# Sketched attention and a two-layer block: a new order for the first chunk, the first weight, chunk 1 and batch 1, and features in two column halves

## The chip, the cores and the metric

The kernel runs on one core of one Trainium2 chip. The metric is the device time of one execution in microseconds (us). Before the change three runs took 143.87, 144.07 and 145.85 us; the median is 144.07.

## The reference

Attention replaces the softmax by products of two sketches; a layer norm and a two-layer block with a residual follow. Inputs are q, k, v of 4 batches, 4 heads, 1088 rows and 32 columns, S1 and S2 of 8 x 32, and weights of 128 x 512 and 512 x 128.

```python
def phi(x):
    a = np.einsum('rd,bhsd->bhsr', S1, x)
    b = np.einsum('rd,bhsd->bhsr', S2, x)
    return np.einsum('bhsi,bhsj->bhsij', a, b).reshape(*x.shape[:-1], r * r)
q_p, k_p = (phi(q), phi(k))
kv = np.einsum('bhsf,bhsd->bhfd', k_p, v)
z = np.sum(k_p, axis=2)
num = np.einsum('bhsf,bhfd->bhsd', q_p, kv)
den = np.einsum('bhsf,bhf->bhs', q_p, z)[..., None] + 1e-06
x = num / den                                # then (B, S, H*D), 128 columns
mu = np.mean(x, axis=-1, keepdims=True)
var = np.mean((x - mu) ** 2, axis=-1, keepdims=True)
xn = (x - mu) / np.sqrt(var + 1e-06) * g_ln
ch = np.maximum(xn @ w_ch1, 0.0) @ w_ch2
out = x + ch
```

The sketches and the weights arrive as 64-bit numbers. The kernel turns them into 32-bit ones with integer and float steps on their two words.

## The kernel before

A batch is 9 tiles of 128 positions-by-head columns for keys. Queries are worked on in 9 chunks: two chunks of four tiles for each batch, and a last one with what is left of all batches. All engines are written in one program order; each engine runs its own instructions in the order of the program and waits on semaphores for the others. There is no planner: the order of the calls at the end of the kernel sets everything.

The steps by name. `turn_k(b, ..)` transposes keys on DVE. `sketches` turns S1 and S2 into the block matrix `sk` (two matmuls and a masked copy), and `sketches2` makes `s2b`. `key_features` multiplies the transposed keys with `sk` on PE (L289) and copies to `fs` on ACT (L291). `key_products` multiplies the two halves of `fs` into `kp`, on POOL or DVE (L298). `key_sums` (L309) and `key_scale` (L323) bring the sum of the key features into the third part of `skq`, the weights with which the queries are multiplied. `key_values` (L329) contracts `kp` with v, `key_rows` copies it, `key_spread` (L344) transposes it into `kvr`.

For a chunk c: `turn_q` transposes queries on DVE (L354), `query_features` multiplies with `skq` into the PSUM bank FB (L372, L377 for the last chunk) and copies to `fq` on ACT (L383). `quotients` (L396 to L401) makes the denominator and divides on DVE, `query_products` (L408) forms `qp`, `query_turn` (L420) transposes it to `qpT`, and `numerators` (L442) contracts it with `kvr` into X and copies to `xT` on ACT (L451). `rows_of` (L459, L461) turns `xT` into rows `x`, and `stats` (L468 to L475) takes mean and variance on DVE and the power on POOL. `hidden(c, j)` (L491, L492) is a quarter of the first layer with its relu on ACT, `second(c, t)` (L500) one tile of the second layer, `finish` (L511) adds the residual and stores.

The first weight is brought into 32 bits by DVE (`split`, `power`), ACT (three float steps) and POOL (`last`), and then multiplied with `cg`, the scale of the layer norm with the mean taken out (L566, L567). The second weight takes the same steps without the product.

PSUM holds X (four banks), M[0] and M[1] (the two layers take turns in them), XP and FB. `fill(n, w)` issues n products of a tile of ones into M[0], whose result nobody reads. In the trace each of these matmuls is two instructions.

The loads stand on one queue (SP's) in the order k of batch 0 in two pieces, w1, q of batch 0, v of batch 0, w2, then the other batches; S1 and S2 stand on ACT's queue, g on POOL's.

Before the change the whole of batch 0's keys, chunk 0 up to the rows, chunk 1 up to its products, both weights, and batch 1's keys up to the scale come ahead of the first `hidden`. From there a loop over the nine chunks mixes the dense layers of chunk c with the features of chunk c + 2, the numerators of chunk c + 1, and the next batch's key work.

Of the kernel before, what the change touches and what calls it, by code (L numbers as in the profile page):

```python
# [25 lines left out]
def kernel(  # L26
# [132 lines left out]
    def fill(n, w):  # L159
        for _ in range(n):  # L160
            pe.matmul(M[0][:, 0:w], ones, ones[:, 0:w], start=True, stop=True)  # L161
# [49 lines left out]
    class weight:  # L211
# [7 lines left out]
        def split(self):  # L219
            if not self.plain:  # L220
                split(self.t)
                t = self.t
                act.activation(t["exf"], t["ex"], AF.Relu, bias=m896)
                act.activation(t["mant"], t["bits"], AF.Identity, bias=one, scale=2.0**-20)
                act.activation(t["low"], t["lo"], AF.Copy, scale=2.0**-52)

        def power(self):
            if not self.plain:
                power(self.t, P)

        def last(self, eng=None):
            t = None if self.plain else self.t
            if self.plain:
                pool.tensor_copy(out=self.dst, in_=self.raw)
            else:
# [1 line left out]
                pool.tensor_tensor(out=self.dst, in0=t["mant"], in1=t["e3"].bitcast(F32),
                                   op=ALU.mult)
# [17 lines left out]
    def sketches():  # L256

        for i in range(2):
            pe.matmul(FB[:, R * i : R * (i + 1)],
                      s_f[:, DM * i : DM * (i + 1)], ident[0:R, 0:R],  # L260
                      start=True, stop=True)
        dve.tensor_tensor(
            out=_ap(sk, 0, P, 0, [[HR, 2], [R, H], [1, R]]),
            in0=_ap(FB, 0, P, 0, [[R, 2], [0, H], [1, R]]),
            in1=_ap(m32, 0, P, 0, [[0, 2], [1, H], [0, R]]),
            op=ALU.mult,
        )
# [18 lines left out]
    def key_features(b, t0, t1, bank):  # L286
        base = 512 * bank - W * t0
        for t in range(t0, t1):
            pe.matmul(X[:, base + W * t : base + W * (t + 1)],  # L289
                      kT[b % 2][:, P * t : P * (t + 1)], sk, start=True, stop=True)  # L290
        act.copy(  # L291
            _ap(fs[b % 2], 0, P, HR * t0, [[HR, t1 - t0], [KB, 2], [1, HR]]),
            _ap(X, 0, P, base + W * t0, [[W, t1 - t0], [HR, 2], [1, HR]]),
# [11 lines left out]
    def key_sums(b, o=1536):  # L305
        f = fs[b % 2]
        for t in range(NT):
            c = t % 4
            pe.matmul(  # L309
                X[32 * c : 32 * c + 32, o : o + 32],  # L310
# [11 lines left out]
    def key_scale(b, o=1568):  # L322
        pe.matmul(X[:, o : o + 32], s2b, zT, start=True, stop=True)  # L323
        dve.tensor_copy(out=skq[b][:, W : W + HR], in_=X[:, o : o + HR])  # L324
# [43 lines left out]
    def query_features(c):  # L368
        n = tiles(c)
        if c < 8:  # L370
            for t in range(n):
                pe.matmul(FB[:, WQ * t : WQ * (t + 1)], qT[c][:, P * t : P * (t + 1)],  # L372
                          skq[c // 2], start=True, stop=True)
        else:
            for t in range(n):
                for i in range(2):
                    pe.matmul(  # L377
# [284 lines left out]
```

## Time and profile before

| | |
|---|---|
| median of three runs | 144.07 us |
| the profiled execution | 144.32 us |
| its span, first to last instruction | 142.5 us |
| PE busy | 121.7 us, 85% of the span |
| DVE, ACT, POOL busy | 62.1, 43.7, 51.0 us |
| mean granted TensorE clock | 0.891 |
| first `hidden` product starts at | 42.69 us |

The profiled execution's own time is 1.8 us above its span; sums made on the trace have to be compared with 144.32 and not with the median. Busy PE time is modelled from pipelined matmuls, so it shows where PE has work and not how well it is used. A row of the timeline gives the start, the time from its first instruction's start to its last one's end, engine, line, and in brackets the idle time ahead and what ended it. The granted clock is a separate column of the windows.

### The profile page before, as it was taken

The page shows a single profiled execution, that of the slowest core. Times are in us where ns is not written, and L with a number is a line of the kernel's source. Part 1 is how long each engine was busy: PE and PEld are TensorE (multiplying, and loading weights), DVE is VectorE, ACT ScalarE, POOL GpSimd, SP SyncE. Part 2 cuts the span into 40 slices and gives each one's busy share as a digit, 9 for nine tenths or more (in the row PEclk, how much of TensorE's full clock was granted, in tenths as well). Part 3 has the DMA queues.
Part 4 walks back from the last instruction along what each step waited for, and adds up shares of the span by engine and source line. Part 5 has one row for each costly group of instructions (what it writes and reads, how often), then busy time and mean ns, then how long its engine had stood idle before and what let it go on. Part 6 is the DMA issues. An engine that isn't in the chain of part 4 may idle for free. (4 is left out here: it accounts for less than half of the span.)

```text
span 142.5 us, 3720 instructions
## 1 busy us (share of the span) xinstructions
PE 121.7 (85%) x1586; PEld 93.6 (66%) x1586; DVE 62.1 (44%) x208; ACT 43.7 (31%) x85; POOL 51.0 (36%) x61
## 2 busy tenths in 40 slices
PE   7789883392579999989999999999999999899750
PEld 7679872262466488569668757965966858569440
DVE  2704377009705558433456653365453544301310
ACT  4011116030611540532253254044236054142310
POOL 6242041605299503373650255545305320302000
PEclk9975589655555999999999999999999999999999
DMA  4899999980000000300020030020011030030111
GB/s 144 252 248 288 227 295 243 266 205 13 0 0 2 0 5 5 74 0 5 18 55 5 4 77 0 0 60 25 0 40 38 2 74 5 0 78 0 45 33 35
DMA packets 6273, 10.21 MB, mean 72 GB/s; under 512 B 1136, under 2 KB 3952, under 8 KB 6256
## 3 DMA queue, kind: packets, MB, share of 16 engines
q1 hardware_dynamic: 6000, 9.90, 27.9%
q8 instruction: 12, 0.20, 0.6%
q10 hardware_dynamic: 224, 0.07, 0.2%
q14 instruction: 5, 0.04, 0.1%
q0 software_dynamic: 32, 0.00, 0.0%
HBM read 7.74 MB, written 2.23 MB: 70 GB/s over the span
## 5 line engine op out<-in xcount | busy, mean ns | idle before, releaser
L491 PE MATMUL M<-xT,w 128*128 128x512 f32 (+1 forms) x72 | 37.5, 612 | 1.2 <-DVE ob L511 1.2
L492 ACT ACTIVATE hT<-M 128x512 f32<-128x512 f32 (+1 forms) x36 | 20.7, 574 | 49.6 <-PE M L491 49.5
L500 PE MATMUL M<-w,hT 128*128 128x128 f32 x272 | 33.4, 277 | 0.0
L500 PEld LDWEIGHTS M<-w,hT 128*128 128x128 f32 x272 | 31.8, 192 | 0.2
L408 POOL TENSOR_TENSOR qp<-a,fq 128x1024 f32<-128x1024 f32 (+1 forms) x9 | 16.2, 1803 | 35.2 <-DVE a L401 35.2
L289 PE MATMUL X<-sk,kT 128*128 128x64 f32 x72 | 12.5, 334 | 6.8 <-ACT fs L291 3.0
L289 PEld LDWEIGHTS X<-sk,kT 128*128 128x128 f32 x72 | 11.6, 244 | 8.7 <-ACT fs L291 3.6
L298 POOL TENSOR_TENSOR kp<-fs 128x1024 f32<-128x1024 f32 (+1 forms) x7 | 15.0, 2148 | 5.5 <-ACT fs L291 5.5
L491 PEld LDWEIGHTS M<-xT,w 128*128 128x128 f32 x72 | 11.6, 198 | 6.2 <-issue 2.6
L511 DVE SCALAR_TENSOR_TENSOR ob<-M,rstd,x 128x128 f32<-128x128 f32 x34 | 9.6, 343 | 13.8 <-PE M L500 9.8
L420 DVE STREAM_TRANSPOSE qpT<-qp 128x1024 f32<-128x1024 f32 (+1 forms) x10 | 10.7, 1079 | 10.6 <-POOL qp L408 10.6
L468 DVE BATCH_NORM_STATS2 st<-x 128x6 f32<-128x128 f32 x34 | 7.4, 278 | 15.9 <-ACT x L461 15.9
L372 PEld LDWEIGHTS FB<-skq,qT 128*128 128x128 f32 x64 | 10.8, 243 | 4.0 <-issue 3.3
L473 POOL TENSOR_SCALAR va<-mv 128x4 f32<-128x4 f32 (+1 forms) x9 | 2.1, 230 | 30.4 <-DVE mv L470 25.0
L442 PEld LDWEIGHTS X<-qpT,kvr 32*32 32x32 f32 x640 | 7.1, 103 | 8.5 <-issue 6.7
L442 PE MATMUL X<-qpT,kvr 32*32 32x128 f32 (+1 forms) x640 | 10.3, 262 | 1.3 <-DVE qpT L420 0.9
L372 PE MATMUL FB<-skq,qT 128*128 128x96 f32 x64 | 10.8, 327 | 0.4 <-DVE skq L324 0.4
L396 DVE TENSOR_TENSOR ac<-FB,fq 128x128 f32<-128x128 f32 (+1 forms) x9 | 2.6, 284 | 16.8 <-ACT fq L383 16.8
L161 PE MATMUL M<-ones 128*128 128x128 f32 x40 | 8.6, 390 | 1.0 <-DVE m L125 1.0
L475 POOL TENSOR_TENSOR rstd<-va,mhalf 128x4 f32<-128x4 f32 (+1 forms) x9 | 9.0, 1003 | 0.8
L161 PEld LDWEIGHTS M<-ones 128*128 128x128 f32 x40 | 7.7, 292 | 1.3 <-DVE m L125 1.0
L459 PEld LDWEIGHTS XP<-ident,xT 128*128 128x128 f32 x34 | 4.7, 151 | 5.4 <-issue 5.4
(80 smaller groups left out, 100.8 us busy)
## 6 DMA issues: line engine op xcount, KB each, us to landing
qn<-in_q_dram SPq DMA_DIRECT2D x4, 544.0 KB, 8.4
out_dram<-ob SPq DMA_DIRECT2D x32, 64.0 KB, 1.7
kn<-in_k_dram SPq DMA_DIRECT2D x3, 544.0 KB, 11.3
vn<-in_v_dram SPq DMA_DIRECT2D x8, 144.0 KB, 8.6
w_raw<-in_moe_w_ch_dram SPq DMA_DIRECT2D x2, 512.0 KB, 6.1
vn<-in_v_dram SPq DMA_DIRECT2D x8, 128.0 KB, 7.9
kn<-in_k_dram SPq DMA_DIRECT2D x1, 288.0 KB, 2.9
kn<-in_k_dram SPq DMA_DIRECT2D x1, 256.0 KB, 3.0
```

What stands on the lines that cost most here:

```text
L161: pe.matmul(M[0][:, 0:w], ones, ones[:, 0:w], start=True, stop=True)
L289: pe.matmul(X[:, base + W * t : base + W * (t + 1)], kT[b % 2][:, P * t : P * (t + 1)], sk, start=True, stop=True)
L298: eng.tensor_tensor(out=_ap(o, 0, P, H * F * t0, [[F, (t1 - t0) * H], [R, R], [1, R]]), in0=_ap(f, 0, P, HR * t0, [[R, (t1 - t0) * H], [1, ...
L372: pe.matmul(FB[:, WQ * t : WQ * (t + 1)], qT[c][:, P * t : P * (t + 1)], skq[c // 2], start=True, stop=True)
L408: eng.tensor_tensor(out=_ap(qp[c], 0, P, H * F * t0, [[F, m], [R, R], [1, R]]), in0=_ap(a2s[c], 0, P, H * R * t0, [[R, m], [1, R], [0, R]] ...
L420: dve.transpose(_ap(qpT[c], 0, P, 32 * t0, [[32, t1 - t0], [32 * n, 8], [1, 32]]), qp[c][:, t0 * H * F : t1 * H * F],)
L442: pe.matmul(X[D * h : D * h + D, o : o + 32 * m], kv[rows, DM * i + D * h : DM * i + D * h + D], t[rows, src : src + 32 * m], start=(i == ...
L475: pool.tensor_tensor(out=rs[:, 0:n], in0=va[:, 0:n], in1=mhalf[:, 0:n], op=ALU.pow)
L491: pe.matmul(hp[:, 0:n], w1[:, P * j : P * (j + 1)], xT[c][:, 0:n], start=True, stop=True)
L492: act.activation(hT[c][:, 512 * j : 512 * j + n], hp[:, 0:n], AF.Relu)
L500: pe.matmul(po[c][:, DM * t : DM * (t + 1)], hT[c][:, 512 * j + P * t : 512 * j + P * (t + 1)], w2[:, DM * j : DM * (j + 1)], start=(j == ...
L511: dve.scalar_tensor_tensor(out=ob[:, P * t : P * (t + 1)], in0=po[c][:, P * t : P * (t + 1)], scalar=rstd[c][:, t : t + 1], in1=x[c][:, P ...
```

## The change

*Features in two column halves.* A tile's 128 columns are multiplied as two matmuls of 64 columns that write the two halves of the partitions, in `key_features` and `query_features`. `key_features` of batches 1 to 3 is one block with one copy to `fs`; batch 0's two parts go to M[0] and M[1].

*Start.* S2 is loaded on SP's queue ahead of k, and q of batch 0 ahead of w1. `sketches` writes X in place of FB, and stands between the two key transposes. `cg` is made on POOL at the start, ahead of the four copies of `sk` into `skq`, which now stand ahead of the key products. Batch 0's key products all run on POOL, in three parts.

*First chunk.* Ones are multiplied at more places, 64 instructions in place of 40. `key_values` of batch 0 is cut into three parts with ones between them. `query_products(0)` runs on DVE in four instructions that read one factor from FB, so `fq` of chunk 0 needs only half its copy. `skq` and batch 0's `kvr` are copied by ACT.

*First weight.* It is split after zT and finished in two halves of 256 columns; `mean_free` multiplies each half with `cg`. The second half comes behind the first `hidden`.

*Chunk 1 and batch 1.* `hidden(0, 0)` follows the numerators of chunk 0. What stood ahead of it (chunk 1's features, rows of chunk 0, the second weight, batch 1's keys) is written between the dense products of chunks 0 and 1, by hand. The loop starts with chunk 2.

```diff
-    for i, src in enumerate((S1, S2)):
-        act.dma_start(out=s_raw[:, D * i : D * (i + 1)], in_=src)
+    act.dma_start(out=s_raw[:, 0:D], in_=S1)
+    nc.sync.dma_start(out=s_raw[:, D : 2 * D], in_=S2)
...
+    load_rows(qn, q, 0)
     nc.sync.dma_start(out=w1_raw, in_=moe_w_ch1)
-    load_rows(qn, q, 0)
...
-    def fill(n, w):
+    def fill(n, bank, w=P):
         for _ in range(n):
-            pe.matmul(M[0][:, 0:w], ones, ones[:, 0:w], start=True, stop=True)
+            pe.matmul(bank[:, 0:w], ones, ones[:, 0:w], start=True, stop=True)
...
-    def key_features(b, t0, t1, bank):
-        base = 512 * bank - W * t0
+    def key_features(b, t0=0, t1=NT, bank=None):
+        y = X if bank is None else bank
         for t in range(t0, t1):
-            pe.matmul(X[:, base + W * t : base + W * (t + 1)],
-                      kT[b % 2][:, P * t : P * (t + 1)], sk, start=True, stop=True)
+            for c in range(2):
+                pe.matmul(
+                    y[64 * c : 64 * c + 64, W * (t - t0) : W * (t - t0 + 1)],
+                    kT[b % 2][:, P * t + 64 * c : P * t + 64 * c + 64], sk,
+                    start=True, stop=True,
+                )
...
-        dve.tensor_copy(out=skq[b][:, W : W + HR], in_=X[:, o : o + HR])
+        act.copy(skq[b][:, W : W + HR], y[:, o : o + HR])
...
+        for t in range(n):
+            for i in range(2):
+                src, w = (qT[c], skq[c // 2]) if c < 8 else (qTr, skq[2 * t + i])
+                pe.matmul(
+                    FB[64 * i : 64 * i + 64, WQ * t : WQ * (t + 1)],
+                    src[:, P * t + 64 * i : P * t + 64 * i + 64], w,
+                    start=True, stop=True,
+                )
...
+    def mean_free(a, n, bank):
+        pe.matmul(bank[:, 0:n], cg, w1g[:, a : a + n], start=True, stop=True)
+        act.copy(w1[:, a : a + n], bank[:, 0:n])
+
+    pool.tensor_scalar(out=cg, in0=ident, scalar1=-1.0 / DM, scalar2=g_raw,
+                       op0=ALU.add, op1=ALU.mult)
+    fill(7, FB)
     turn_k(0, 0)
+    sketches()
     turn_k(0, 2)
...
-    for c in range(9):
+    for c in range(2, 9):
```

Three places of the new order, as each engine has them. The first is PE in the first chunk, from the key sums of batch 0 to the numerators of chunk 0: before,

```order
L309 MATMUL X<-fs_201 32x32 x9
L161 MATMUL M_70<-ones 128x128 x4
L323 MATMUL X<-zT,s2b 128x32
L372 MATMUL FB<-skq_197,qT 128x96 x4
L329 MATMUL X<-kp_203,vn_87 32x64 x36
L161 MATMUL M_70<-ones 128x128 x2
L344 MATMUL X<-ident,kvT 128x128 x2
L161 MATMUL M_70<-ones 128x128 x4
L442 MATMUL X<-qpT,kvr_207 32x128 x32
```

and now, from the query features on,

```order
L392 MATMUL FB<-skq_197,qT 64x96 x8
L161 MATMUL XP<-ones 128x128 x4
L344 MATMUL X<-kp_203,vn_87 32x64 x16
L161 MATMUL XP<-ones 128x128 x3
L344 MATMUL X<-kp_203,vn_87 32x64 x12
L161 MATMUL XP<-ones 128x128 x3
L344 MATMUL X<-kp_203,vn_87 32x64 x8
L161 MATMUL XP<-ones 128x128 x2
L360 MATMUL M_70<-ident,kvT 128x128 x2
L161 MATMUL XP<-ones 128x128 x2
L561 MATMUL M_71<-w1g,cg 128x256
L161 MATMUL XP<-ones 128x128 x2
```

The key values (L329, now L344) are in three parts with products on ones between, and the first half of the weight's product stands ahead of the numerators. The second place is PE behind the numerators of chunk 0: before,

```order
L442 MATMUL X<-qpT,kvr_207 32x128 x32
L566 MATMUL M_71<-w1g,cg 128x512
L459 MATMUL XP<-ident,xT 128x128 x4
L372 MATMUL FB<-skq_197,qT 128x96 x4
L289 MATMUL X<-sk,kT_148 128x64 x9
L309 MATMUL X<-fs_202 32x32 x9
L323 MATMUL X<-zT,s2b 128x32
L491 MATMUL M_71<-xT,w_177 128x512
```

and now

```order
L467 MATMUL X<-qpT,kvr_207 32x128 x32
L161 MATMUL XP<-ones 128x128 x2
L516 MATMUL M_71<-xT,w_177 128x512
L392 MATMUL FB<-skq_197,qT 64x96 x8
L561 MATMUL XP<-w1g,cg 128x256
L516 MATMUL M_70<-xT,w_177 128x512
L484 MATMUL XP<-ident,xT 128x128 x4
L516 MATMUL M_71<-xT,w_177 128x512
L516 MATMUL M_70<-xT,w_177 128x512
L301 MATMUL X<-sk,kT_148 64x64 x18
L467 MATMUL X<-qpT,kvr_207 32x128 x32
```

The first dense product (L491, now L516) stands two rows behind the numerators; batch 1's key features (L289, now L301) stand behind all four. The third place is DVE from the quotients of chunk 2 on, where qT holds the transposed queries of chunk 3: before,

```order
L396 TENSOR_TENSOR ac_157<-FB,fq 128x16x8
L398 TENSOR_REDUCE den<-ac_157 128x16
L400 RECIPROCAL rden<-den 128x16
L401 TENSOR_TENSOR a_465<-FB,rden 128x128
L354 STREAM_TRANSPOSE qT<-qn_84 128x4x4x32
L360 STREAM_TRANSPOSE qTr<-qn_84 128x64
L420 STREAM_TRANSPOSE qpT<-qp 128x4x8x32
L468 BN_STATS st<-x 128x6 x4
L470 BN_AGGR mv<-st 128x2 x4
```

and now

```order
L412 TENSOR_TENSOR ac_157<-FB,fq 128x16x8
L414 TENSOR_REDUCE den<-ac_157 128x16
L416 RECIPROCAL rden<-den 128x16
L417 TENSOR_TENSOR a_587<-FB,rden 128x128
L493 BN_STATS st<-x 128x6 x4
L495 BN_AGGR mv<-st 128x2 x4
L373 STREAM_TRANSPOSE qT<-qn_84 128x4x4x32
L412 TENSOR_TENSOR ac_158<-FB,fq 128x16x8
L414 TENSOR_REDUCE den<-ac_158 128x16
L416 RECIPROCAL rden<-den 128x16
L417 TENSOR_TENSOR a_625<-FB,rden 128x128
L445 STREAM_TRANSPOSE qpT<-qp 128x4x8x32
```

The statistics of chunk 1 stood behind chunk 2's products; now they stand ahead of the transposed queries of chunk 3 (L354, now L373), and the quotients of chunk 3 stand ahead of the transpose of chunk 2's products (L420, now L445).

More of the change, by code (lines that the diff above doesn't have):

```diff
@@ L267, in sketches @@
         )
+        for b in range(B):
+            pool.tensor_copy(out=skq[b][:, 0:W], in_=sk)
     def sketches2():
@@ L340, in key_rows, with key_spread @@
         )
-    def key_spread(b):
+    def key_spread(b, y=None, on_act=False):
+        y = X if y is None else y
         for i in range(2):
-            pe.transpose(X[:, P * i : P * (i + 1)], kvT[:, P * i : P * (i + 1)], ident)
-        dve.tensor_copy(out=kvr[b], in_=X[:, 0 : 2 * DM])
+            pe.transpose(y[:, P * i : P * (i + 1)], kvT[:, P * i : P * (i + 1)], ident)
+        if on_act:
+            act.copy(kvr[b], y[:, 0 : 2 * DM])
+        else:
+            dve.tensor_copy(out=kvr[b], in_=y[:, 0 : 2 * DM])
     qT = {}
@@ L549 @@
     query_features(0)
+    W1.floats(1, 0, 256)
+    W1.floats(2, 0, 256)
+    W1.power(0, 256)
     quotients(0)
[L551 to L564 removed]
+    fill(4, XP)
@@ L565 @@
+    key_values(0, 0, 4)
+    fill(3, XP)
+    W1.floats(0, 256, 256)
+    key_values(0, 4, 7)
+    fill(3, XP)
+    W1.floats(1, 256, 256)
+    W1.floats(2, 256, 256)
+    key_values(0, 7, 9)
+    W1.last(0, 256)
+    query_products(0, dve)
+    query_turn(0)
+    key_rows()
+    fill(2, XP)
+    key_spread(0, M[0], on_act=True)
+    fill(2, XP)
+    mean_free(0, 256, M[1])
+    fill(2, XP)
     numerators(0)
-    pe.matmul(M[1], cg, w1g, start=True, stop=True)
-    act.copy(w1, M[1])
+    W1.power(256, 256)
@@ L579 @@
-    W2.last()
-    key_features(1, 0, 4, 0)
-    key_features(1, 4, 9, 1)
-    key_products(pool, 1, 0, 4)
-    key_products(pool, 1, 4, 9)
-    key_sums(1)
-    key_scale(1)
-    turn_q(2)
-    stats(0)
-    for c in range(9):
+    key_features(1)
+    query_turn(1)
+    numerators(1)
+    key_products(pool, 1, 0, 4)
+    stats(0)
+    second(0, 0)
+    key_sums(1, X, 1536)
+    second(0, 1)
+    rows_of(1)
+    key_products(pool, 1, 4, 9)
+    second(0, 2)
+    key_scale(1, X, 1568)
+    turn_q(2)
@@ new lines @@
+    turn_q_rest(0)
+    second(0, 3)
+    query_features(2)
+    finish(0)
+    quotients(2)
+    query_products(2, pool)
+    stats(1)
+    hidden(1, 0)
+    turn_q(3)
+    query_features(3)
+    quotients(3)
+    query_products(3, pool)
+    hidden(1, 1)
+    query_turn(2)
+    key_values(1)
+    key_rows()
+    hidden(1, 2)
+    key_spread(1)
+    turn_k(2, 0)
+    turn_k(2, 2)
+    hidden(1, 3)
+    numerators(2)
+    second(1, 0)
+    key_features(2)
+    key_products(pool, 2, 0, 4)
+    second(1, 1)
@@ L590 @@
+    rows_of(2)
+    stats(2)
+    key_sums(2, X, 1536)
+    second(1, 2)
+    key_products(pool, 2, 4, 9)
+    query_turn(3)
+    key_scale(2, X, 1568)
+    turn_q(4)
+    turn_q_rest(1)
+    second(1, 3)
+    finish(1)
+    for c in range(2, 9):
         nb = c // 2 + 1 if c % 2 == 0 else c // 2 + 2
@@ L596 @@
             quotients(c + 2)
-            query_products(c + 2, pool, 0, tiles(c + 2))
+            query_products(c + 2, pool)
         hidden(c, 1)
```

157 lines of the change are left out of this document (80 added, 77 removed).

## The prediction

> **What bounds the kernel now.** The chain of waits ends in two output steps and unexplained issue time (3% of the span), so it says nothing of the middle. I read the windows instead, cut where the TensorE clock changes. The columns after the length are busy time with instruction counts for PE, weight loads, DVE, ACT and POOL, then the granted clock.
>
> ```profile
> 5.54:8.95 3.41, 1.87 (x14) 1.54 (x13) 1.74 (x4) 0.37 (x1) 0.02 (x1) 1.00 1.00 273
> 15.78:19.19 3.41, 3.41 (x79) 3.07 (x79) 1.58 (x5) 0.46 (x2) 0.33 (x1) 0.50 1.06 269
> 19.19:22.60 3.41, 2.51 (x69) 2.15 (x70) 2.72 (x7) 0.29 (x1) 1.17 (x1) 1.00 1.07 262
> ...
> 26.02:42.69 16.67, 9.93 (x53) 8.04 (x53) 6.19 (x13) 4.12 (x8) 7.50 (x5) 0.50 0.35 82
> 43.08:46.49 3.41, 3.41 (x11) 2.33 (x11) 1.67 (x10) 0.60 (x2) 3.24 (x3) 0.50 0.01 2
> 68.65:132.00 63.35, 62.53 (x937) 45.80 (x936) 28.47 (x104) 23.49 (x45) 22.02 (x20) 1.00 0.11 27
> ```
>
> From 68.65 to 132 PE is busy 62.53 of 63.35 us at full clock: PE is the bound there, and only less PE work helps. From 26.02 to 42.69 PE idles 6.7 us and works the rest at half clock. That stretch is the target. PE's own timeline there, and the first matmul of chunk 2's dense block:
>
> ```profile
> 27.23 2.08 PE L566 MATMUL M<-w1g,cg 128*128 128x512 f32 x2 [3.66 <-POOL w1g L237]
> 29.10 1.06 PE L459 MATMUL XP<-ident,xT 128*128 128x128 f32 x4
> 29.95 1.86 PE L372 MATMUL FB<-skq,qT 128*128 128x96 f32 x8
> 34.83 1.97 PE L289 MATMUL X<-sk,kT 128*128 128x64 f32 x8 [3.02 <-DVE kT L245]
> 38.45 2.39 PE L289 MATMUL X<-sk,kT 128*128 128x64 f32 x10 [1.65 <-ACT fs L291]
> 41.35 0.53 PE L309 MATMUL X<-fs 128*32 128x32 f32 x18 [0.52 <-ACT fs L291]
> 42.24 0.63 PE L323 MATMUL X<-zT,s2b 128*128 128x32 f32 x2 [0.35 <-DVE zT L315]
> 42.69 1.20 PE L491 MATMUL M<-xT,w 128*128 128x512 f32 x1
> ...
> 68.65 1.02 PE L491 MATMUL M<-xT,w 128*128 128x512 f32 x2
> ```
>
> PE waits 3.66 us for the first weight, then for batch 1's keys; the first dense product stands at 42.69, the first of chunk 2 at 68.65. The change puts the first dense product right behind chunk 0's numerators, and spreads batch 1's key work between the dense products of chunks 0 and 1. So I sum three pieces: T0, the new time of that first product; from T0 to chunk 2's first; and from there to the end.
>
> **T0.** The prologue's rows:
>
> ```profile
> 1.04 4.63 PE L161 MATMUL M<-ones 128*128 128x128 f32 x20 [1.04 <-DVE m L125]
> ...
> 4.33 0.18 DVE L174 TENSOR_SCALAR bitss<-s_raw 8x64 uint32<-8x64 uint32 x1 [1.11 <-DMA s_raw<-in_S_dram]
> ...
> 7.33 1.10 PE L289 MATMUL X<-sk,kT 128*128 128x64 f32 x8 [0.72 <-DVE sk L262]
> ...
> 14.97 1.99 PE L372 MATMUL FB<-skq,qT 128*128 128x96 f32 x8 [0.38 <-DVE skq L324]
> 16.89 2.15 PE L329 MATMUL X<-kp,vn 128*32 128x64 f32 x72
> ...
> 19.83 1.06 PE L161 MATMUL M<-ones 128*128 128x128 f32 x8
> 21.79 0.98 PE L442 MATMUL X<-qpT,kvr 32*32 32x128 f32 x55 [0.90 <-DVE qpT L420]
> ```
>
> A product on ones is two instructions: 0.23 us each at low clock (4.63/20), 0.13 at full (1.06/8). Two DMA queues carry S1 and S2 instead of one in turn; I take 0.5 us off (between nothing and 0.9), so S is there at 3.8, and the unchanged 1.5 us of DVE gives sketch matmuls at 5.3. Seven fills end at 4.3, the sketches at 5.9, four more fills (8 x 0.23) at about 7.6, when both key transposes are done. S2 ahead of k delays each later load by one issue, under half a us; q ahead of w1 puts w1 back by one load (4 x 1088 x 32 four-byte numbers, 2 us at the windows' 270 GB/s); w1 is first read behind zT, at 11.3 below, and what hides both is the features' chain. Were w1 later than that, the weight's half steps would come later by as much.
>
> Key features are now 36 half instructions. Bounds at low clock: 1.1 us (the 32-column pace, 2.15/72) to 4.3 (18 at the whole width's 0.24, 2.39/10 at 38.45); I take 2.1, nearer the column-tiled row. They end at 9.7, their copy at 10.2 (0.43, below); key sums, zT, the scale product and its copy, 0.5+0.3+0.6+0.2 with gaps, start query features at 12.3 (14.97 before: two DVE steps no longer stand before zT and the skq copy). These take 0.84 to 1.99; I take 1.5, to 13.8. Then DVE, with the prices of this and the next part (a group's row ends in its busy total, the mean ns of one and the idle before):
>
> ```profile
> 17.40 0.29 DVE L396 TENSOR_TENSOR ac<-FB,fq 128x128 f32<-128x128 f32 x1 [1.71 <-ACT fq L383]
> ...
> 18.74 0.69 DVE L408 TENSOR_TENSOR qp<-a,fq 128x512 f32<-128x512 f32 x1
> ...
> 23.36 0.43 DVE L180 TENSOR_SCALAR e2w<-exfw 128x512 uint32<-128x512 f32 x1 [0.79 <-ACT exfw L223]
> 23.82 0.69 DVE L182 SCALAR_TENSOR_TENSOR e3w<-w_raw,e2w 128x512 uint32<-128x512 uint32 x1
> ...
> 52.79 0.87 DVE L468 BATCH_NORM_STATS2 st<-x 128x6 f32<-128x128 f32 x4 [1.28 <-ACT x L461]
> 53.58 0.36 DVE L470 BATCH_NORM_AGGREGATE mv<-st 128x2 f32<-128x6 f32 x4
> ...
> 54.17 1.36 DVE L245 STREAM_TRANSPOSE kT<-kn 128x576 f32<-128x576 f32 x2
> ...
> L420 DVE STREAM_TRANSPOSE qpT<-qp 128x1024 f32<-128x1024 f32 x7 | 8.7, 1243 | 9.3 <-POOL qp L408 9.3
> ...
> L354 DVE STREAM_TRANSPOSE qT<-qn 128x512 f32<-128x512 f32 x8 | 5.6, 701 | 0.0
> ...
> L291 ACT COPY fs<-X 128x320 f32<-128x320 f32 x4 | 1.7, 426 | 7.8 <-PE X L289 7.8
> ...
> 22.61 0.72 ACT L223 ACTIVATE exfw<-exw,m 128x512 f32<-128x512 uint32 x1 [3.13 <-DVE exw L176]
> ...
> 24.40 0.57 ACT L451 COPY xT<-X 128x512 f32<-128x512 f32 x1
> ```
>
> Copy 0.4 (0.43 for more columns), quotients 1.34 (17.40 to 18.74), four products of about 0.43 (0.69 for twice the size, plus overhead), one transpose 1.24: done at 18.5. PE takes longer: from 13.8, ten fills (20 instructions) and 72 of key values, in the order 8, 32, 6, 24, 6, 16. I let the clock return at 19.19 as before: 20.0 (20.6 at low clock, 17.6 at full). Row copy, spread and ACT's kvr copy lead to 21.4, but four fills' instructions, half a weight product (0.45) and four more hold PE to 22.3. Numerators 1.07 and the xT copy 0.57 with latency: **T0 = 24.0**, with 21.6 for full clock from 13.8 and 27.0 for low clock throughout. POOL's three key products and the weight's half steps run beside this.
>
> **From T0 to chunk 2.** Before, 42.69 to 68.65 is 25.96 us, of which 3.80 to 46.49 ran at half clock: 24.1 at full. Moved in, at half their low-clock rows: rows of chunk 0 0.5, query features 1 0.9, half the weight product 0.5, sums and scale 0.6, and batch 1's key features. Rows for the last, and for halves against whole width:
>
> ```profile
> 60.37 1.00 PE L289 MATMUL X<-sk,kT 128*128 128x64 f32 x8
> 61.84 1.33 PE L289 MATMUL X<-sk,kT 128*128 128x64 f32 x10 [0.46 <-ACT fs L291]
> ...
> 104.64 1.03 PE L372 MATMUL FB<-skq,qT 128*128 128x96 f32 x8
> 105.50 0.62 PE L491 MATMUL M<-xT,w 128*128 128x512 f32 x1
> ...
> 114.26 0.55 PE L377 MATMUL FB<-skq,qTr 128*64 128x96 f32 x8
> 114.74 0.70 PE L491 MATMUL M<-xT,w 128*128 128x512 f32 x1
> ```
>
> The last chunk already uses halves: eight take 0.48 to the next product, for two tiles; whole width takes 0.86 for four. Sixteen halves cost 0.48 plus eight at about 0.045 (0.55 less one latency, over seven), 0.84, to 0.96 if simply doubled. So I cost query features at no change. The Trainium skill (TensorEngine Tiling (Array Packing), Tiling Modes) speaks against the change: a change of tiling mode drains the engine. The same page's table allows up to 2x for a dimension of at most 64; by that the four later calls would save 1.7 us in all. By the drain they could cost; the row here has it inside the 0.48.
>
> Key features cost 36 x 0.045 = 1.6 against 2.8 now (60.37 to 63.17, the wait between its parts included); I count 0.7 saved after overheads (0 to 1.5). PE work is then 24.1 + 2.5 + 1.6 - 0.7 = 27.5.
>
> To it come four idle times that the new order makes. (a) Chunk 1's fq copy stands behind the relu and w2's exfw on ACT: T0 + 1.1 + 0.6 + 0.72 + 0.4; then quotients 1.34, w2's e2 and e3 1.12, key transposes 1.36: T0 + 6.65, while PE has 5.4 of work (four dense products, features, half weight, rows): 1.25. (b) Numerators 1 write the bank that the features copy reads; one copy of 576 is about 0.67 by its size: 0.85. (c) Query features 3 need FB free, and on DVE turn_q(3) stands behind quotients 2 and stats 1: 1.1 + 0.4 + 1.34 + 1.23 + 0.70 = 4.75 after query features 2 start, and PE has 1.75 to do: 3.0. All of chunk 1's dense work is queued behind that wait. (d) Batch 2's zT stands behind stats 2: after features 2 come a second-layer tile (1.0, eight instructions of the shape at 19.83), rows 0.55, x copy 0.6, stats 1.23 and zT 0.2, 3.8 with latencies; PE has two such tiles, rows and sums, 2.9: 0.9. Together 6.0, so 33.5 at full clock.
>
> The clock then decides. It changed only on a 3.41 us grid; the window busy 1.87 lost it (the clock is 0.50 after it), the one busy 2.51 kept it, and the full ones at 15.78 and 43.08 regained it. Idle (c) leaves at least one window near or below 1.9. I add one low window, half its length: 1.7. The Trainium skill (TensorE: Matmul & The Clock Gate, Why this matters for your kernels) asks only for no idle gap above about 3 us; the drop at 8.95 disagrees, with 0.72 its longest wait in a row here. By the page the sum would lack the 1.7.
>
> **To the end.** 142.5 - 68.65 = 73.85, less 0.7 for batch 3's key features: 73.15. Sum: 24.0 + 33.5 + 1.7 + 73.15 = 132.4 of span. The profiled execution took 144.32 for a span of 142.5, 1.8 around it: 134.2 us, against a median of 144.07.
>
> **The rivals.** *The clock holds* and PE is dense early: T0 21.6 to 24.0, no low window: 130.1 to 132.5. For it: 2.51 of 3.41 sufficed. Against: (c). *Two low windows and a cold prologue*: 27.0 + 33.5 + 3.4 + 73.15 + 1.8 = 138.9; windows before 15.78 were nearly full and yet low. *No change*: four to seven further low windows between T0 and chunk 2 bring 141 to 146. *Slower*: the gaps keep the clock low from T0 to chunk 2, as it was from 26.02 to 46.49. 27.5 us of PE work at the fills' ratio (0.23/0.13) is 49, which swallows the idle times; with T0 at 27.0 the total is 27 + 49 + 73.15 + 1.8 = 151. It decides from seven low windows on (12 us of gain over 1.7). Against it: the moved-in work stands between dense products like those that regained the clock at 46.49 in one window. That the change fails to do what it says is excluded by the instruction order.
>
> **How the numbers follow.** Forecast with its own spread 132.5 to 136: 0.45. Clock holds: 0.25. Two low windows, 136 to 141: 0.17. No change: 0.08. Slower: 0.05. About 2% (141.2 to 147.0) is what a measurement tells from no change. Faster is 0.87. The range 129.8 to 138.8 leaves out the last two and the edges of the others.
>
> **What would show it.** First dense product at 22 to 27; PE idle near 3 us ahead of query features 3, released by DVE's qT; a key feature block below 2 us at full clock; clock low at most twice after T0; chunk 2's first product at 56 to 62. It is wrong if T0 passes 30, if half features hold PE longer than whole ones did, or if the clock stays low through chunk 0.

## The result and the profile after

The changed kernel takes 134.51 us (median of four executions, 132.65 to 136.16) against 144.01 (143.87 to 145.85): a ratio of 0.924, with a 95% interval of 0.908 to 0.941. Ratios here compare the faster executions of each kernel alone, so they can differ from the ratio of the medians (0.934 here). The executions of one kernel lie up to 3.5 us apart; the section on the prediction says what moves the two of them that were profiled. The profiled execution of after was the longest of the four, 136.16 us for a span of 134.4, 1.8 around it, as before.

The page of after first: PE's busy time, and the clock in 40 slices of 3.36 us. The windows under it are cut on the clock's grid, with the columns that the prediction named; the last one begins at chunk 2's first dense product.

```profile
PE 120.2 (89%) x1748; PEld 88.8 (66%) x1748; DVE 63.6 (47%) x204; ACT 44.7 (33%) x91; POOL 53.5 (40%) x65
...
PEclk9999999998569869999999999999999999999995
```

```profile
12.32:15.73 3.41, 3.41 (x26) 2.96 (x26) 2.80 (x4) 1.35 (x5) 1.93 (x2) 1.00 1.09 291
...
29.37:32.78 3.41, 1.32 (x33) 1.12 (x34) 3.41 (x4) 1.16 (x3) 3.17 (x3) 0.98 1.07 192
32.78:36.19 3.41, 2.68 (x77) 2.00 (x75) 1.18 (x9) 1.15 (x2) 2.19 (x3) 0.50 0.45 119
36.19:39.60 3.41, 3.41 (x33) 3.12 (x33) 1.03 (x3) 0.07 (x1) 3.33 (x3) 0.52 0.02 6
...
43.01:46.42 3.41, 1.17 (x6) 0.30 (x2) 3.23 (x16) 0.97 (x2) 1.39 (x1) 0.98 0.32 77
46.42:49.83 3.41, 3.15 (x18) 1.79 (x18) 1.13 (x5) 0.37 (x1) 1.83 (x3) 0.52 0.00 0
...
61.34:125.00 63.66, 62.89 (x990) 43.96 (x988) 29.66 (x108) 23.84 (x46) 22.96 (x21) 1.00 0.11 27
```

The windows busy 1.32 and 1.17 lose the clock. A window busy 2.68 doesn't bring it back, the full one and the one busy 3.15 do. That makes three low windows behind the first dense product: two from 32.78, one from 46.42. From 61.34 on PE is as full as it was before.

The 1.00 in the first of these windows, and the first digits of PEclk, mislead. The column reads 1.00 until the trace's first record of the clock, which comes at 15.6 here. Ahead of it PE runs at half speed, as the durations show: the query features at 13.43 (below) take 1.55 us, and the same step takes 0.88 at 62.29.

PE's timeline of after, at the places that answer to those of before:

```profile
7.98 2.19 PE L301 MATMUL M<-sk,kT 128*64 128x64 f32 x36
...
13.43 1.55 PE L392 MATMUL FB<-skq,qT 128*64 128x96 f32 x16
...
21.71 1.46 PE L467 MATMUL X<-qpT,kvr 32*32 32x128 f32 x64
...
23.85 1.12 PE L516 MATMUL M<-xT,w 128*128 128x512 f32 x2
...
31.25 0.33 PE L301 MATMUL X<-sk,kT 128*64 128x64 f32 x2 [1.83 <-DVE kT L254]
31.85 1.54 PE L301 MATMUL X<-sk,kT 128*64 128x64 f32 x34 [0.27 <-DVE kT L254]
34.12 1.52 PE L467 MATMUL X<-qpT,kvr 32*32 32x128 f32 x64 [0.73 <-ACT fs L306]
...
46.68 1.55 PE L392 MATMUL FB<-skq,qT 128*64 128x96 f32 x16 [2.50 <-DVE qT L373]
...
55.34 1.27 PE L301 MATMUL X<-sk,kT 128*64 128x64 f32 x36
56.53 1.16 PE L525 MATMUL M<-w,hT 128*128 128x128 f32 x8
...
60.12 0.41 PE L338 MATMUL X<-zT,s2b 128*128 128x32 f32 x2 [0.59 <-DVE zT L330]
...
61.34 1.02 PE L516 MATMUL M<-xT,w 128*128 128x512 f32 x2
```

The first dense product stands at 23.85 (42.69 before), chunk 2's first at 61.34 (68.65 before). So 7.31 us of the span are gained up to there, and 0.79 behind it (73.85 before, 134.4 - 61.34 = 73.06 now). The four waits of the new order are all there, at the places that the prediction named: 1.83 and 0.27 ahead of batch 1's key features, 0.73 ahead of chunk 1's numerators, 2.50 ahead of chunk 3's query features, 0.59 ahead of batch 2's scale product.

DVE of after, at the start, in the first chunk and behind chunk 1's quotients; and then POOL's two instructions beside the long ones:

```profile
3.15 0.20 DVE L174 TENSOR_SCALAR bitss<-s_raw 8x64 uint32<-8x64 uint32 x1
...
12.07 1.25 DVE L174 TENSOR_SCALAR bitsw<-w_raw 128x512 uint32<-128x512 uint32 x1
13.24 1.29 DVE L176 TENSOR_SCALAR exw<-w_raw 128x512 uint32<-128x512 uint32 x1
...
15.77 0.28 DVE L412 TENSOR_TENSOR ac<-FB,fq 128x128 f32<-128x128 f32 x1
...
21.52 0.42 DVE L176 TENSOR_SCALAR exw<-w_raw 128x512 uint32<-128x512 uint32 x1
...
28.19 2.32 DVE L182 SCALAR_TENSOR_TENSOR e3w<-w_raw,e2w 128x512 uint32<-128x512 uint32 x1
30.43 1.36 DVE L254 STREAM_TRANSPOSE kT<-kn 128x576 f32<-128x576 f32 x2
```

```profile
9.61 4.64 POOL L313 TENSOR_TENSOR kp<-fs 128x1024 f32<-128x1024 f32 x3 [2.47 <-ACT fs L306]
...
27.97 2.00 POOL L433 TENSOR_TENSOR qp<-a,fq 128x1024 f32<-128x1024 f32 x1 [6.65 <-ACT hT L517]
```

The second weight's L182 takes 2.32 us; the same step took 0.69 before. It starts inside POOL's product (27.97 to 29.97) and ends 0.54 behind it, which is most of such a step after POOL is done. In the same way L174 and L176 take 1.25 and 1.29 beside POOL's key products, where the second weight's L176 at 21.52, with POOL idle, takes 0.42.

### The profile page after: what moved, and what is told of

Read it like the earlier page. It is cut to its first block, busy times and chain, and to the rows that moved or that the text cites. A ratio compares the mean times of both kernels' runs of the same rounds, so it can differ in the third digit from the quotient of the medians.

```text
span 134.4 us, 4057 instructions
## 1 busy us (share of the span) xinstructions
PE 120.2 (89%) x1748; PEld 88.8 (66%) x1748; DVE 63.6 (47%) x204; ACT 44.7 (33%) x91; POOL 53.5 (40%) x65
## 5 line engine op out<-in xcount | busy, mean ns | idle before, releaser
L516 PE MATMUL M<-xT,w 128*128 128x512 f32 (+1 forms) x72 | 37.2, 610 | 1.3 <-DVE ob L536 1.2
L525 PE MATMUL M<-w,hT 128*128 128x128 f32 x272 | 36.0, 286 | 0.0
L525 PEld LDWEIGHTS M<-w,hT 128*128 128x128 f32 x272 | 33.5, 199 | 0.9 <-issue 0.6
L517 ACT ACTIVATE hT<-M 128x512 f32<-128x512 f32 (+1 forms) x36 | 20.7, 575 | 38.3 <-PE M L516 38.2
L433 POOL TENSOR_TENSOR qp<-a,fq 128x1024 f32<-128x1024 f32 (+1 forms) x8 | 14.8, 1849 | 28.4 <-DVE a L417 21.8
L313 POOL TENSOR_TENSOR kp<-fs 128x1024 f32<-128x1024 f32 (+3 forms) x9 | 17.7, 1976 | 9.8 <-ACT fs L306 9.8
L516 PEld LDWEIGHTS M<-xT,w 128*128 128x128 f32 x72 | 11.5, 192 | 7.4 <-issue 2.7
L493 DVE BATCH_NORM_STATS2 st<-x 128x6 f32<-128x128 f32 x34 | 7.4, 279 | 15.5 <-ACT x L486 15.5
L445 DVE STREAM_TRANSPOSE qpT<-qp 128x1024 f32<-128x1024 f32 (+1 forms) x9 | 10.6, 1178 | 7.7 <-POOL qp L433 7.7
L392 PEld LDWEIGHTS FB<-skq,qT 128*64 128x64 f32 x128 | 6.7, 158 | 7.4 <-issue 7.3
L498 POOL TENSOR_SCALAR va<-mv 128x4 f32<-128x4 f32 (+1 forms) x9 | 2.1, 230 | 23.3 <-DVE mv L495 21.6
L392 PE MATMUL FB<-skq,qT 128*64 128x96 f32 x128 | 8.4, 282 | 2.5 <-DVE qT L373 2.5
L161 PE MATMUL FB<-ones 128*128 128x128 f32 x28 | 7.8, 449 | 1.0 <-DVE m L125 1.0
L161 PEld LDWEIGHTS FB<-ones 128*128 128x128 f32 x28 | 6.4, 327 | 1.2 <-DVE m L125 1.0
L476 ACT COPY xT<-X 128x512 f32<-128x512 f32 (+1 forms) x9 | 5.1, 562 | 6.3 <-PE X L467 6.3
L486 ACT COPY x<-XP 128x512 f32<-128x512 f32 (+1 forms) x9 | 5.0, 559 | 5.0 <-PE XP L484 5.0
```

Of the source, the lines that this page charges most:

```text
L161: pe.matmul(bank[:, 0:w], ones, ones[:, 0:w], start=True, stop=True)
L313: eng.tensor_tensor(out=_ap(o, 0, P, H * F * t0, [[F, (t1 - t0) * H], [R, R], [1, R]]), in0=_ap(f, 0, P, HR * t0, [[R, (t1 - t0) * H], [1, ...
L392: pe.matmul(FB[64 * i : 64 * i + 64, WQ * t : WQ * (t + 1)], src[:, P * t + 64 * i : P * t + 64 * i + 64], w, start=True, stop=True,)
L433: eng.tensor_tensor(out=_ap(p, 0, P, 0, [[F, m], [R, R], [1, R]]), in0=_ap(a2s[c], 0, P, 0, [[R, m], [1, R], [0, R]]), in1=_ap(fq[c], 0, P ...
L445: dve.transpose(_ap(qpT[c], 0, P, 32 * t0, [[32, t1 - t0], [32 * n, 8], [1, 32]]), qp[c][:, t0 * H * F : t1 * H * F],)
L493: dve.bn_stats(out=st[:, 6 * t : 6 * t + 6], in_=x[c][:, P * t : P * (t + 1)])
```

## The experiments

All were timed in three rounds, four executions each, beside the kernel before. The four groups had medians of before of 144.19, 145.20, 143.99 and 144.80, so the ratios compare better than the times. Products on ones are read by nobody; the kernels that drop some of them compute the same.

### The change again, and its two halves apart

The first run repeats the changed kernel as it is. The second has its order, with the whole-width features of before; the third has the order of before, with features in halves. The core of the second's edit:

```diff
-            for c in range(2):
-                pe.matmul(
-                    y[64 * c : 64 * c + 64, W * (t - t0) : W * (t - t0 + 1)],
-                    kT[b % 2][:, P * t + 64 * c : P * t + 64 * c + 64], sk, ...)
+            pe.matmul(y[:, W * (t - t0) : W * (t - t0 + 1)],
+                      kT[b % 2][:, P * t : P * (t + 1)], sk, start=True, stop=True)
```

The third makes the opposite edit in the kernel before; both also change `query_features` in the same way.

> The changed kernel once more, to see how the clock's grid falls. Theory of the prediction (order and waits set the time, the clock adds 1.7 us for each low window): the first dense product again at 23.5 to 24.5, PE idle 2 to 3 us ahead of query features 3; chunk 2's first product between 57.5 and 62 according to one to three low windows, the rest 73 us; 132 to 136.5 us in all. Rival (the clock is the same in every execution): runs within 0.5 us of each other.

> The changed kernel with its features in whole width again (one product of 128 columns in place of two of 64), order kept. Theory: query features cost the same either way; key features 1.2 to 1.4 us more for each batch where PE is the bound (batch 3 for certain, batches 1 and 2 where no wait hides it) and 1 to 2 us in the first chunk: 2.5 to 5 us slower than the changed kernel, 136.5 to 140. Rival (halves are most of the gain): 8 us slower or more. Rival (mode changes eat what halves save): within 1 us.

> The kernel before with features in two halves and nothing else. Theory: 0.7 to 1.2 us for each of batches 2 and 3, and the low-clock features of batches 0 and 1 shorter by 1 to 2 us each, part of it hidden: 140 to 142.5. Rival (halves are most of the gain): 137 or less. Rival (nothing): 144.

Measured: the change again 135.36 us, ratio 0.934 [0.925, 0.943]; the new order alone 140.15, 0.968 [0.961, 0.976]; the halves alone 140.49, 0.969 [0.959, 0.978]. Whole width is thus 4.8 us slower than the change, within the 2.5 to 5 expected. Each part is worth 3.2% by itself, 6.3% as a sum, and together they give 6.6%: they add up. Half of the gain is the halves', which the prediction had not said. PE's rows of the new order at whole width:

```profile
8.04 3.69 PE L300 MATMUL M<-sk,kT 128*128 128x64 f32 x18 [1.32 <-DVE kT L254]
...
14.85 1.98 PE L387 MATMUL FB<-skq,qT 128*128 128x96 f32 x8
...
25.76 0.70 PE L515 MATMUL M<-xT,w 128*128 128x512 f32 x1
...
80.88 2.12 PE L300 MATMUL X<-sk,kT 128*128 128x64 f32 x18
82.84 1.08 PE L515 MATMUL M<-xT,w 128*128 128x512 f32 x2
```

In the first chunk, at low clock, the key features take 3.69 where halves take 2.19, and the query features 1.98 where halves take 1.55. Both lie on the chain to the first dense product, which stands at 25.76 against 23.85 in after and 21.71 in its repeat. Part of these distances is the clock, which came back in the first chunk at 18.8, 15.6 and 10.2 in the three traces. At full clock a key block holds PE for 1.96 (80.88 to 82.84) against 1.19 (55.34 to 56.53). Of the drop from 2.63 before (60.37 to 63.00) about 0.7 is thus the one block with one copy, and 0.8 the halves.

Behind chunk 2's first product the halves are worth little all the same: 73.19 at whole width, 73.06 in halves. The reason stands in the query features: from chunk 4's to chunk 5's it is 11.11 us at whole width (65.97 to 77.08) and 11.21 in halves (62.29 to 73.50). Four such calls at 0.1 give back half of what batch 3's key block saves.

The halves alone, in the order before, show something else in chunk 0's numerators:

```profile
18.73 0.50 PE L450 MATMUL X<-qpT,kvr 32*32 32x128 f32 x29 [1.24 <-DVE qpT L428]
21.97 1.06 PE L450 MATMUL X<-qpT,kvr 32*32 32x128 f32 x35 [2.75 <-issue]
```

PE stops for 2.75 us in the middle of a step, and no semaphore releases it. Before, the same place shows 0.37 us:

```profile
23.15 0.42 PE L442 MATMUL X<-qpT,kvr 32*32 32x128 f32 x9 [0.37 <-issue]
```

In both the stop stands behind the 221st row of a matmul in PE's program. So the halves reach that place 3.5 us earlier (19.23 against 22.77), and 2.4 of these are lost there.

### The ones

The fourth kernel drops the products on ones behind the first seven.

```diff
-    fill(4, FB)
     key_features(0, 0, 4, M[0])
...
-    fill(4, XP)
     key_values(0, 0, 4)
-    fill(3, XP)
```

(And so on through the first chunk.)

> The changed kernel with only the first seven products on ones; the other 25 are left out, which changes no result. Theory (the ones hold or regain the clock, and PE's serial order costs about 2 us): PE falls to half clock in the first chunk, the first dense product comes at 22 to 25 and runs at half clock, one to three more low windows: 134 to 139. Rival (the ones only take PE's time): the transposed products at 19.8 set the numerators, first dense product at 22, 132 or less.

Measured 135.11 us, 0.932 [0.924, 0.941], the same as the change. Its PE at the numerators:

```profile
18.10 1.42 PE L467 MATMUL X<-qpT,kvr 32*32 32x128 f32 x52 [0.17 <-DVE qpT L445]
23.08 0.67 PE L467 MATMUL X<-qpT,kvr 32*32 32x128 f32 x12 [3.56 <-issue]
```

Without ones the numerators start at 18.10 instead of 21.71, so the ones do hold PE up, as the prediction's 22.3 said. But PE stops again at its 221st matmul, for 3.56 us, and the first dense product comes at 24.45. It runs at half clock (2.08 us), as the theory said: the clock is low from 8.45 to 28.93. So what the ones cost on PE, and what the wait and the low clock cost without them, happen to be equal here.

### The waits of the new order

Three moves on DVE alone: chunk 3's query transpose ahead of chunk 2's quotients; batch 1's key transposes ahead of the first dense product; and both of these, with the statistics of chunk 2 behind batch 2's zT as well. PE's program stays as it is. The third:

```diff
+    turn_k(1, 0)
+    turn_k(1, 2)
     hidden(0, 0)
...
-    turn_k(1, 0)
-    turn_k(1, 2)
     key_features(1)
...
     turn_q_rest(0)
+    turn_q(3)
...
     hidden(1, 0)
-    turn_q(3)
     query_features(3)
...
-    stats(2)
...
     key_scale(2, X, 1568)
+    stats(2)
```

> The changed kernel with the transpose of chunk 3's queries moved ahead of chunk 0's output step on DVE; nothing else. Theory (idle time (c) is that transpose, queued behind chunk 1's statistics): PE's wait ahead of query features 3 falls from 2.5 us to 1.0 or less, and with it one low window may go: 1.5 to 3.5 us faster than the changed kernel, 132 to 134. Rival (another engine is late there anyway): no change, the wait stands under another name.

> The changed kernel with batch 1's key transposes moved ahead of chunk 1's quotients on DVE, which idles there for 4.5 us. Theory (idle time (a)): PE's 1.8 us ahead of batch 1's key features goes, numerators 1 then wait for the transposed products, 2.3 us earlier than now; with the low windows behind it 2 to 5.5 us faster, 130 to 133.5. Rival (w2's steps set the end of this stretch): no change, since the second layer waits for w2 instead.

> Both of the former, and batch 2's key sums read ahead of chunk 2's statistics on DVE. Theory (the waits of the new order and the low windows they bring are what is left between first dense product and chunk 2): the stretch falls from 37.5 us to 30 to 32, with no low window in most executions: 126.5 to 130.5. Rival (the clock falls whatever the waits): 131 to 133.

Measured: the query transpose alone 131.00 us, 0.897 [0.885, 0.909], faster than the 132 to 134 expected; the key transposes alone 131.51, 0.898 [0.888, 0.908]; all three 127.18, 0.879 [0.868, 0.890]. The waits that stay, PE's row of the first, and then of the second kernel:

```profile
40.63 0.88 PE L392 MATMUL FB<-skq,qT 128*64 128x96 f32 x16 [0.84 <-DVE a L417]
```

```profile
29.73 1.06 PE L467 MATMUL X<-qpT,kvr 32*32 32x128 f32 x64 [1.19 <-DVE qpT L445]
```

The first takes 1.66 off the wait of 2.50; what is left waits for chunk 2's own quotients, which hold FB. The second removes 2.10 and moves 0.46 to the numerators, now behind the turned products. From its first dense product to chunk 2's, the first kernel takes 34.40 us (19.46 to 53.86) and the second 33.18 (21.76 to 54.94), where the change takes 37.49. That is 3.1 and 4.3 less for about 1.6 us less of waiting in each; the rest is PE's busy time, 31.58 us in the change for the same work, 30.14 and 28.72 here. The kernel with all three shows the same, PE's rows first and then the stretch from its first dense product to chunk 2's:

```profile
29.50 1.07 PE L467 MATMUL X<-qpT,kvr 32*32 32x128 f32 x64 [1.44 <-DVE st L493]
...
38.21 0.88 PE L392 MATMUL FB<-skq,qT 128*64 128x96 f32 x16 [0.84 <-DVE a L417]
...
50.58 1.02 PE L516 MATMUL M<-xT,w 128*128 128x512 f32 x2
```

```profile
21.28:50.58 29.30, 27.02 (x457) 19.76 (x458) 17.99 (x51) 12.58 (x25) 18.61 (x13) 1.00 0.39 97
```

Idle falls from 5.9 to 2.3 us, no window is low any more, and the stretch takes 29.30 in place of 37.49: 3.6 us of waits, and 4.6 of busy time. The clock accounts for the 4.6: in the change the three low windows hold 9.24 us of busy time (2.68, 3.41 and 3.15), half of which is 4.6. The whole is some 7 us faster than the change, and ahead of both kernels by the medians, though the intervals overlap a little.

### The slow DVE steps

Is it POOL's product that makes L182 long? This kernel moves the second weight's L180 and L182 ahead of chunk 1's quotients, so that POOL's product, which needs those, comes later.

```diff
     query_features(1)
+    W2.power()
     quotients(1)
...
     W2.floats(2)
-    W2.power()
     W2.last()
```

> The changed kernel with w2's two power steps on DVE ahead of chunk 1's quotients, where POOL is idle, in place of beside POOL's products of chunk 1. Theory (the second of them, e3, took 2.32 us and not 0.69 because it ran beside a POOL instruction): it takes 0.7 us, batch 1's key features start about 1.5 us earlier, 1 to 3 us faster than the changed kernel, 132.5 to 134.5. Rival (the long row has another cause): 2.3 us again and no gain.

Measured 131.55 us, 0.913 [0.907, 0.919]. DVE's row of the step, and POOL's product:

```profile
26.34 0.70 DVE L182 SCALAR_TENSOR_TENSOR e3w<-w_raw,e2w 128x512 uint32<-128x512 uint32 x1
```

```profile
28.40 1.96 POOL L433 TENSOR_TENSOR qp<-a,fq 128x1024 f32<-128x1024 f32 x1 [7.08 <-DVE a L417]
```

With POOL idle the same instruction takes 0.70. The wait of 1.83 for batch 1's keys is gone (0.27 is left); 0.93 stands ahead of the numerators, and 2.48 is still ahead of chunk 3's query features. So one DVE step beside a POOL product is worth some 2 to 3 us of the total here (0.913 against 0.924 and 0.934); the interval overlaps that of the first measurement of the change and lies below that of the second. Every other kernel with the new order has the long row too, 2.32 or 2.33 beside POOL's product; before and the halves alone, where POOL is idle at the step's start, have 0.69. The three moves of the last section and this one were not run together. The Trainium skill (SBUF — State Buffer, SBUF: two separate sides) says that DVE and GpSimd take turns on a shared pair of ports, with an exclusive lock for a whole instruction, when a DVE instruction with two SBUF inputs meets a GpSimd one that reads SBUF, or when the DVE instruction runs in a two-port mode. L182 has two such inputs, and its rows agree, 2.32 against 0.70.

### The wait at the 221st matmul

With DVE's waits gone, are the ones still worth nothing? The first of these kernels drops the later ones from the version with all three moves. The second also holds the loads of batches 2 and 3 back: a one-column write into a tile that they fill, behind the turn of chunk 0's products. The third holds those loads back but keeps the ones.

```diff
     query_turn(0)
+    dve.memset(kn[2][:, 0:1], 0.0)
+    for b in range(2, B):
+        load_rows(kn, k, b)
+        load_v(b)
+        load_rows(qn, q, b)
```

> The last one with only the first seven products on ones. Theory (PE cannot go past the 221st matmul of its program before 20 to 23 us, because the next block of instructions is loaded behind the input loads; in the four earlier traces PE's unexplained wait comes at exactly that matmul): a wait without a releaser inside the numerators of chunk 0 until 21.5 to 23.5, and a time within 1.5 us of the kernel with the ones. Rival (the ones hold the clock): 2 us slower or more. Rival (the ones only cost PE time): 2 us faster.

> The kernel with three waits removed and only the first seven products on ones, and the loads of batches 2 and 3 held back until chunk 0's products are transposed (a write of one column into k of batch 2 by DVE, which the load then overwrites, stands ahead of them). Theory (PE waits at its 221st matmul for instructions that queue behind the input loads): without those loads the wait of 3.9 us falls below 1 us and the first dense product comes at 20.5 to 22.5 in place of 25.3: 126 to 129. Rival (the wait is of another kind, as its place alone was the evidence): the wait stays near 3.9 and the time near 130.8.

> The kernel with three waits removed, all products on ones, and the loads of batches 2 and 3 held back in the same way. Theory: it hardly waits for instructions now, so only little comes, 125.5 to 127.5; against the last kernel it tells what the ones themselves do once instructions are there in time: within 1.5 us means that they do little for the clock. Rival (the ones hold the clock): 2 us or more faster than the last kernel.

Measured: no ones 130.76 us, 0.900 [0.891, 0.910]; with late loads 130.47 (126.82 to 131.88, without a ratio); late loads with ones 128.33, 0.885 [0.876, 0.894]. Here the ones are worth 3.6 us, against the 1.5 at most that were expected; the rival, that the ones hold the clock, had 2 or more. PE without ones:

```profile
19.09 0.96 PE L467 MATMUL X<-qpT,kvr 32*32 32x128 f32 x52 [0.23 <-DVE qpT L445]
23.97 0.67 PE L467 MATMUL X<-qpT,kvr 32*32 32x128 f32 x12 [3.92 <-issue]
25.34 2.08 PE L516 MATMUL M<-xT,w 128*128 128x512 f32 x2 [0.71 <-ACT xT L476]
```

PE waits for 3.92 us, and the product behind it runs at half clock (2.08), so this pair of runs doesn't tell the wait from the clock. With the loads of batches 2 and 3 held back the wait is still 3.19, and the time is that of the rival. But the queue wasn't empty: the engines that move data were still full, with batch 1's loads (the last two columns of this window of it are their share and GB/s). With the ones in, holding these loads back gains nothing (128.33 against 127.18).

```profile
16.00:18.00 2.00, 1.52 (x19) 0.91 (x8) 1.93 (x6) 0.83 (x3) 1.27 (x2) 1.00 1.11 165
```

So the last kernel, without ones, also holds back q and v of batch 1. Only batch 0, both weights and k of batch 1 are asked for earlier.

```diff
     load_rows(kn, k, 1)
-    load_v(1)
-    load_rows(qn, q, 1)
...
     query_turn(0)
+    dve.memset(qn[1][:, 0:1], 0.0)
+    load_rows(qn, q, 1)
+    load_v(1)
```

(The loads of batches 2 and 3 follow there.)

> This is the version without the later products on ones, with the loads of q of batch 1, v of batch 1 and everything behind them held back until the quotients of step 0 have been turned, so that only k, q and v of batch 0, w1, w2 and k of batch 1 are asked for before that. Theory (TensorE's instructions at the 221st matmul queue behind the input loads): with the queues empty there the wait of 3.9 us falls below 1 us, the first dense product stands at 20.5 to 22 in place of 25.3, and the time is 126 to 128.5 us. Rival (the wait has nothing to do with the loads' traffic): it stays above 3 us, and the time is 130 to 131 us.

Measured 127.48 us (125.37 to 128.48), 0.871 [0.861, 0.882], whose interval lies below that of the kernel without ones. PE at the numerators, and the window ahead of them:

```profile
18.93 1.52 PE L461 MATMUL X<-qpT,kvr 32*32 32x128 f32 x64 [1.01 <-DVE qn L589]
21.12 2.08 PE L510 MATMUL M<-xT,w 128*128 128x512 f32 x2 [0.68 <-ACT xT L470]
```

```profile
16.00:18.00 2.00, 1.54 (x4) 0.82 (x4) 1.93 (x6) 0.74 (x4) 1.24 (x2) 1.00 0.00 0
```

No data moves from 16 to 18, the numerators run through without a stop, and the first dense product stands at 21.12 instead of 25.34. Both run at low clock (2.08 us for the product, 1.13 at full); the 1.00 in these windows again stands ahead of the first record of the clock, which comes at 27.0 in this trace. So the wait at that matmul depends on the input loads in flight.

What PE waits for there shows in the packets of the DMA queues. Queue 8 carries packets of 16 KB that the trace calls instructions: 12 in the traces with 1586 and 1612 rows of matmuls, 13 in those with 1698 to 1748, so they go with PE's program. In the kernel without ones, one of them falls between 8 and 26 us:

```profile
q8 instruction: 1, 0.02, 0.4%
```

With narrower windows of the same view its start can be found, and compared with the time at which PE gets to its 221st matmul, the one at which it stops, and goes on (all in us):

| kernel | packet starts | PE gets there | PE goes on |
|---|---|---|---|
| before | 20.2 | 22.77 | 23.15 |
| the change | 19.4 | 21.9 | 22.2 |
| halves alone | 19.5 | 19.23 | 21.97 |
| the change without ones | 20.3 | 19.52 | 23.08 |
| three moves without ones | 21.3 | 20.05 | 23.97 |
| the same with late loads | 20.7 | 20.36 | 23.55 |
| the same with a quiet queue | 14.0 | 19.8 | no stop |
| three moves with ones | 15.5 | 19.6 | no stop |

In all six stops (that of the change is 0.31 us, inside a row) PE goes on 2.5 to 2.9 us after the packet's start, whenever PE itself arrived. In the eight kernels without a stop the packet starts 3.1 to 5.8 us before PE gets there. So PE waits for its next instructions, and they come late. What delays the packet is shown only in part: with the queue quiet it starts at 14.0, without ones and with loads in flight at 20.3 to 21.3, and with ones at 15.5 though loads are in flight then too. So the ones help where the packet is early, and why it is early with them stays open. With the wait gone the ones are worth nothing again: this version and the one with ones and all three moves can't be told apart (127.48 and 127.18).

## Why the prediction was right, and where it was not

The time, 134.51 us against 134.2, lies at the middle of the range, and that is in part luck. The 134.2 was added up for a profiled execution, and the one of after took 136.16. Most of the 2.0 between them is the clock behind T0. By the prediction's own pieces:

| piece | predicted | measured |
|---|---|---|
| T0, first dense product | 24.0 | 23.85 |
| from there to chunk 2: PE work at full clock | 27.5 | 27.0 |
| idle (a), (b), (c), (d) | 1.25, 0.85, 3.0, 0.9 | 2.10, 0.73, 2.50, 0.59 |
| low clock in that stretch | 1.7 | about 4.5 |
| from chunk 2 to the end | 73.15 | 73.06 |
| span | 132.4 | 134.4 |

The 27.0 is from the kernel with all three moves, which has PE's program of the change and ran that stretch at full clock. The 4.5 is what is left of 37.49 after it and 5.92 of idle; half the busy time of the three low windows, 4.6, agrees with it.

**T0** came out at 23.85, between bounds of 21.6 and 27.0, by errors that cancel. S came 1.2 us earlier (3.15 against 4.33), not 0.5. The query features started at 13.43, not 12.3, and took 1.55 for 1.5; the key features took 2.19 for 2.1. The quotients started at 15.77 instead of 14.2: 1.1 of it comes from the late features, the rest from the first weight's steps ahead of them on DVE, whose split took 2.5 us beside POOL's key products and not 0.84. "POOL's three key products and the weight's half steps run beside this" had it free. Against all this, the clock came back at 15.6 and not at the 19.19 of before, so PE's key values and ones ended sooner than the 22.3 given to them: the numerators start at 21.71. The repeat shows how much of that is chance:

```profile
12.45 0.88 PE L392 MATMUL FB<-skq,qT 128*64 128x96 f32 x16
...
21.71 1.13 PE L516 MATMUL M<-xT,w 128*128 128x512 f32 x2
```

There the clock came back at 10.2, the query features take 0.88, and T0 is 21.71, the full-clock bound. The return of the clock alone moves T0 by 2 us from one execution to the next.

**The idle times** are the right four, with the right releasers, and their sum is right to 0.1 (5.92 for 6.0). Term (a) was mis-sized: "w2's e2 and e3 1.12" measured 2.74 beside POOL's product.

**The clock** was counted too low: one low window, and there were three, 4.5 us in place of 1.7. This is the term of the sum that was mis-sized most. From T0 on the rule itself held: windows busy below 1.9 lost it, full ones and one at 3.15 regained it. In the first chunk it doesn't hold: PE is busy throughout the windows from 5.50 to 15.73 and stays at half speed until 15.6, and before, the full window from 8.95 didn't bring the clock back either. Nor is there one bound for losing it: a window busy 2.69 lost it in the kernel with late loads and ones (9.45 to 12.86), one busy 1.97 kept it in the kernel with three moves (26.73 to 30.14). Between T0 and chunk 2, every window at full clock that was busy less than 1.6 lost it, in all the traces. But (a) also left such a window, once its DVE step was long, and a window busy 2.68, which would have kept the clock, didn't bring it back. By the Trainium skill (TensorE: Matmul & The Clock Gate, Why this matters for your kernels), which asks for no idle gap above about 3 us, the clock would hold here; waits of 1.83 and 2.50 lost it, so the trace disagrees. After and its repeat both have three low windows in this stretch (37.49 and 37.58 us); their spans, 134.4 and 132.3, differ by T0. What moved the executions that were not profiled isn't known.

**The halves.** "Query features at no change" holds: from the dense product ahead of them to the one behind, 1.76 against 1.73, and about 0.1 lost from one call to the next. The drain that the prediction weighed is no more than that. Key features saved 1.4 a block (2.63 to 1.20 for batches 2 and 3), not 0.7: that term was mis-sized. Batch 3's block saves 0.7 more than counted, and yet the end came out at 73.06, since the four query features took about 0.4 back and 0.2 went elsewhere. What the prediction left unsaid is that half of the whole gain would go if the halves were undone; it had the halves' prices in T0, but not as a share.

**The rivals.** *The clock holds* came true only in experiments, when the waits were gone: 127.18, below its 130.1, because the idle times that break the clock went too. *Two low windows and a cold prologue* was right in kind: three windows fell low, and the prologue was cold until 15.6. Its 138.9 is too long because it had the prologue cold to the end (27.0). *Slower* needed seven low windows; there were three.

## What to carry to other kernels

Price a wait on PE by the clock too: here taking away 3.6 us of waits made the stretch 8.2 us shorter, since each of the two windows of 3.41 us that were busy 1.32 and 1.17 cost the next one or two their clock. Check the clock by durations where the column may stand ahead of its first record. Before a DVE step is put beside work of POOL, look in the trace for the same step alone and beside POOL; a factor of three was hidden in two places here. When halves and order are changed at once, run each alone: the sum was right, but half of it came from a part that had been counted at little (0.7 us a key block, nothing for the later query features).
